# Turning two heads of k and q as 64x128 tiles beside the scores, in an attention and mixer kernel on one core

## The chip, the core and the metric

The kernel runs on one core of one Trainium2 chip. The metric is the time of one execution in microseconds, taken on the device. The text calls the core's engines by the names of the profile: PE multiplies matrices (PEld is its weight loads), DVE is the vector engine, ACT the scalar engine, POOL and SP issue most of the DMAs, and POOL does a little arithmetic as well.

## The reference

Eight batches of eight heads, 576 positions, 64 elements a head. Attention has a causal mask and a bias that falls with the running sum of `max(s, 0)`; a mixer over tokens and one over channels follow.

```python
scores = scale * np.matmul(q, k.transpose(0, 1, 3, 2))
cum = np.cumsum(np.maximum(s, 0.0), axis=-1)
bias = -(cum[:, :, :, None] - cum[:, :, None, :])
scores = np.where(causal, -1000000000.0, scores + np.minimum(bias, 0.0))
attn = softmax(scores)
x = heads side by side of np.matmul(attn, v)          # 8 x 576 x 512
h = np.maximum(x^T @ w_tok1, 0.0) @ w_tok2            # over tokens, 256 wide
u = x + h^T
out = u + np.maximum(u @ w_ch1, 0.0) @ w_ch2          # over channels, 1536 wide
```

## The kernel before

The bias is taken as a weight on v, `exp(cum)` of a position, so that a position's window of attention is its own block of 128 and the one before. A test at the end sets a flag for inputs where this does not hold; a general path, not taken here, would then compute everything anew.

**Stages of a batch.** Heads come in groups of four (`quad`, two groups a batch, numbered 0 to 15 in this text). k and q of a group are loaded as bf16 into a buffer of the ring `qkn` (5 buffers), two heads on the upper and two on the lower 64 partitions, 9 positions a partition. PE turns them: for k and then for q (`ti`), 9 slices x 2 halves x 2 heads, 36 transposes of 64x64 (line 706). Each result, two heads stacked on 128 partitions, is copied by ACT (line 718) or DVE (line 720) to `kT` or `qT`. A group has two pairs of heads (`pair`). A pair's scores are ten matmuls (line 750) on tiles of 64 rows and 128 columns, the two heads of the pair beside each other on the upper and the lower rows, in two pieces: 4 matmuls into one psc buffer and 6 into another. ACT exponentiates each piece (line 758), DVE masks it (lines 767 and 775), PE multiplies it with v (line 821), DVE divides (lines 850 and 854). When a batch has its eight heads, `tok` runs the token mixer (lines 921, 983) and turns its result: from batch 2 on by DMA transposes on SP's queue (line 999). `chan` runs the channel mixer (lines 1039 and 1064) with an evacuation by ACT (line 1046) or DVE (line 1048) per output of the first half, and stores each block.

**Buffers that PE writes.** `psc` has two buffers of 1024 columns, `pmx` four of 512. Before, the turns of batch 0 go to pmx, those of the other batches to one psc buffer for each `ti`; scores and attention times v use psc; both mixers use pmx.

**The order.** `Plan.op` records every piece of work with its engines, durations, priority, and what it reads, writes and holds. `Plan.run` then places them greedily: at each step it takes the engine that could start earliest, and on it, of the operations that could start within a small slack, the one with the lowest priority number. On PE it knows two shapes of tile: an operation with `mode=1` (turns and scores) has narrow tiles, and a change between narrow and full costs `SWITCH = 0.095` (line 17); while PE is in narrow shape, narrow work that is ready goes first. `after` makes an operation wait for the end of another on its engine. `late` and the `MARGIN` constants put a reserve between producer and consumer. The order found becomes the order of instructions of each engine, which the chip follows with semaphores. Up to `WARM` = 45 us, idle PE time is filled with matmuls on zeros (line 1160).

**Loads.** POOL issues the loads of k, q, v and weights in one chain (`load_op`), the first in a paced manner, by touching a piece of an earlier load (line 459). A load of k and q needs a free `qkn` buffer. At batch 5 (`B - 3`), POOL touches the turned input of the channel mixer before the loads of two batches' k and q come again for the sums of squares that the flag needs (`stage_sq`); the other batches' squares are ACT operations of low priority (line 664). The scan of line 1123 and the small operations behind it belong to that flag as well; they wait for the key `late`, set in `tok(0)`.

Of the kernel before, what the change touches and what calls it, by code (L numbers as in the profile page):

```python
# [237 lines left out]
def c_pe(n, f32=False):  # L238
    occ = n * (4 if f32 else 1) / 2400.0 + 0.0025
    return occ, occ + 0.21  # L240
# [131 lines left out]
def kernel(  # L372
# [22 lines left out]
    NQ = 512  # L395
    LAG = 2.5
    WARM = 45.0
    TOK = 2.0
    R = 9
    PR = S // R  # L400
# [9 lines left out]
    def ring(name, n, shape, dt, pool=None):  # L410
        p = pool or fast
        return Ring(name, [p.tile(shape, dt, name=f"{name}{i}", tag=f"{name}{i}") for i in range(n)])
# [17 lines left out]
        return EB[jc] + (64 if odd else 128) if jc == NJ - 2 else EB[jc] - (64 if odd else 0)  # L430

    r_qn = ring("qkn", 5, [128, 2, 2, R * D], BF16)
    r_qT = ring("qT", 4, [128, S], BF16)
    r_kT = ring("kT", 4, [128, 640], BF16)
    r_E = ring("E", 4, [128, 2, EW], BF16)
# [97 lines left out]
    for ti, src in enumerate((k, q)):  # L533
        def load0(ti=ti, src=src):
            nc.sync.dma_start(out=stage[:, ti, :, :],
                              in_=src[0, 0:4, :, :].rearrange("(f e) (p r) d -> (e p) f (r d)", e=2, r=R))
        P.op({"SP": (0.6, 4.0 + 0.9 * ti, load0)}, writes=[("stage", ti)], prio=-9 + ti)
        for f in range(2):
            def cast0(eng, ti=ti, f=f):
                if eng:  # L540
                    nc.vector.tensor_copy(out=first.t[:, ti, f, :], in_=stage[:, ti, f, :])
                else:
                    nc.scalar.copy(out=first.t[:, ti, f, :], in_=stage[:, ti, f, :])
            P.op({"ACT": (*c_act(576), lambda cast0=cast0: cast0(0)),
                  "DVE": (0.1 + 576 * 0.00104, 0.25 + 576 * 0.00104, lambda cast0=cast0: cast0(1))},
                 reads=[("stage", ti)], writes=[(first, ti, f)], prio=-6)
# [120 lines left out]
    def stage_qk(b, h):  # L667
        n = qkn[(b, h)] = Buf(r_qn)
        for i, src in enumerate((k, q)):
            load_cast(n, b, h, i, src)  # L670
        if b > 1:
            squares(b, h, n)
# [13 lines left out]
    xbuf = {}  # L686
    bd = Buf(r_mx, False)

    def quad(b, h):
        nat = qkn[(b, h)]  # L690
        np_ = (b * H + h) / 2
        dsts = [(Buf(r_kT), Buf(r_qT)) for e in range(2)]
        pads = [("pad", 2), ("pad", 3)] if b == 0 and h == 4 else []
        for ti in range(2):
            pts = [Buf(r_mx, False) for e in range(2)] if b == 0 else [Buf(r_sc, False)] * 2

            def pv(e, pts=pts):
                o = pts[e].t[:, :].bitcast(BF16)
                return o[:, 0:1024] if b == 0 else o[:, e * 1024 : e * 1024 + 1024]

            def tr(ti=ti, pv=pv):
                for r in range(R):
                    for e in range(2):
                        p0 = e * PR
                        for f in range(2):
                            nc.tensor.transpose(out=pv(e)[f * D : f * D + D, r * PR : (r + 1) * PR],  # L706
                                                in_=nat.t[p0 : p0 + PR, ti, f, r * D : (r + 1) * D],
                                                identity=ident[p0 : p0 + PR, p0 : p0 + PR])
            turn = P.op({"PE": (R * 0.031, R * 0.031 + 0.21, tr)}, reads=([(nat, ti, 0), (nat, ti, 1)] if b == 0 and h == 0 else [(nat, ti)]) + ["ident"] + pads,
                 writes=[(pts[e], e) for e in range(2)] + (["turned"] if b == 0 and h == 0 and ti == 0 else []), holds=[d[ti] for d in dsts], prio=(np_ - 30 * (b < 1 and h < 1), 2), mode=1)  # L710
            if b == 0 and h == 0 and ti == 1:
                scan.deps.add(turn)
            for e in range(2):
                def ev(eng, ti=ti, e=e, pv=pv):
                    i = pv(e)[:, 0:S].rearrange("d (r p) -> d p r", r=R)
                    o = dsts[e][ti].t[:, 0:S].rearrange("d (p r) -> d p r", r=R)
                    if eng == 0:
                        nc.scalar.copy(out=o, in_=i)  # L718
                    else:
                        nc.vector.tensor_copy(out=o, in_=i)  # L720
                P.op({"ACT": (*c_act(576), lambda ev=ev: ev(0)), "DVE": (*c_dve(576), lambda ev=ev: ev(1))},
                     reads=[(pts[e], e)], writes=[(dsts[e][ti], 0)], prio=1, alone=pts[e])
        for e in range(2):
            pair(b, h + e, *dsts[e])

    def pair(b, h, kT, qT):
        np_ = (b * H + h // 4 * 4) / 2 + h % 2
        E = Buf(r_E)
        odd = b % 2
        for pc, piece in enumerate(PIECES):  # L730
            ps = Buf(r_sc, False)
            c0 = 0
            cols = []
            for (jc, a, e) in piece:
                cols.append((jc, a, e, c0))
                c0 += e - a

            if b == 0:
                def preset(ps=ps, pc=pc):
                    for hh in range(2):  # L740
                        nc.tensor.matmul(out=ps.t[:, hh * 512 : hh * 512 + 512], lhsT=ident[:, :], rhs=neg[:, pc, :],  # L741
                                         start=True, stop=False)
                P.op({"PE": (2 * c_pe(512)[0], 2 * c_pe(512)[0] + 0.21, preset)}, reads=["neg", "ident"] + ["turned"],
                     writes=[(ps, 0)], prio=(np_ - 9, 0))

            def mm(ps=ps, cols=cols):
                for (jc, a, e, c0) in cols:
                    j0 = S - 128 if odd and jc == NJ - 1 else jc * 128
                    for hh in range(2):
                        nc.tensor.matmul(out=ps.t[:, hh * 512 + c0 : hh * 512 + c0 + e - a],  # L750
                                         lhsT=kT.t[hh * 64 : hh * 64 + 64, j0 : j0 + 128],
                                         rhs=qT.t[hh * 64 : hh * 64 + 64, a:e], start=b > 0, stop=b > 0 or jc == cols[-1][0])
            occ = sum(c_pe(e - a)[0] for (_, a, e, _) in cols)
            P.op({"PE": (occ, occ + 0.21, mm)}, reads=[(kT, 0), (qT, 0)], writes=[(ps, 0)], holds=[E], prio=(np_ - 9 * (b < 1), 1),
                 mode=1)

            def ex(ps=ps, pc=pc):
                nc.scalar.activation(out=E.t[:, :, 512 * pc : 512 * pc + 512],  # L758
                                     in_=ps.t[:, :].rearrange("p (e n) -> p e n", e=2), func=AF.Exp, scale=0.125)
            P.op(act(1024, ex), reads=[(ps, 0)], writes=[(E, jc) for (jc, a, e) in piece], prio=0)  # L760

            if b == 0:
                continue

            def mk(pc=pc):
                o = E.t[:, :, 512 * pc : 512 * pc + 512].rearrange("p e (c n) -> p e c n", c=2)[:, :, :, 0:128]
                nc.vector.tensor_tensor(  # L767
                    out=o, in0=o, in1=keep[:, :].unsqueeze(1).unsqueeze(1).to_broadcast([128, 2, 2, 128]), op=ALU.mult)
            P.op(dve(512, mk, True), reads=[(E, piece[0][0]), (E, piece[1][0]), "keep"],
                 writes=[(E, piece[0][0]), (E, piece[1][0])], prio=0, lock=True)  # L770
            if pc == 1:
                def mk4():
                    k0 = 64 if odd else 0
                    o = E.t[:, :, EB[4] : EB[4] + 64]
                    nc.vector.tensor_tensor(
                        out=o, in0=o, in1=keep[:, k0 : k0 + 64].unsqueeze(1).to_broadcast([128, 2, 64]), op=ALU.mult)
                P.op(dve(128, mk4, True), reads=[(E, 4), "keep"], writes=[(E, 4)], prio=0, lock=True)
# [117 lines left out]
    def tok(b):  # L895
# [80 lines left out]
        for c in range(NJ):  # L976
# [40 lines left out]
                else:  # L1017
                    nc.vector.tensor_copy(out=o, in_=i)
            P.op(either(512, lambda ev=ev: ev(0), lambda ev=ev: ev(1), True), reads=[(pt, 0)], writes=[(uT, c)], prio=0)
        if b == 0:  # L1020
            P.writer["late"] = P.ops[-1]
        return u, us, uT

# [80 lines left out]
    for i in range(2, 4):  # L1104
        load_ch2(i)
    stage_v(1)
    for b in range(2, B):
        stage_qk(b, 0)
        stage_v(b)
        stage_qk(b, 4)  # L1110
    for b in range(B):
        for h in range(0, H, 4):
            quad(b, h)
        st = tok(b)
        chan(b, *st)
        if b == B - 3:
            for c in range(NJ):
                touch(lambda c=c, uT=st[2]: uT.t[0:1, 0, c * 128 : c * 128 + 1], [(st[2], c)], 1)
            for i in range(2):
                for h in range(0, H, 4):  # L1120
                    stage_sq(i, h)
# [87 lines left out]
```

## Time and profile before

| | us |
|---|---|
| median of 3 runs | 303.14 |
| lowest and highest of them | 301.69 and 303.29 |
| the profiled execution, its own time | 302.87 |
| its span in the profile | 301.1 |
| PE busy in it | 292.5 |
| DVE, ACT, POOL busy | 187.5, 183.9, 80.6 |

The runs are timed from outside of the program, the span runs from the first to the last instruction of the profile. Rows of the timeline have the start, the length, the engine, the line, the operation, the tiles that it writes and reads, the tile shape of PE, the operand's size and how many instructions are merged. On PE the length takes in the pipeline's end of the last matmul, so what an instruction costs the stream is read from start to start. Groups of instructions have busy time and mean duration in ns of one.

### The profile page before, as it was taken

How to read it: one execution, taken by the hardware profiler on the slowest of the kernel's cores; microseconds unless marked ns; L12 is line 12 of the kernel's file. 1: busy time of each engine (PE TensorE's matmuls, PEld its weight loads, DVE VectorE, ACT ScalarE, POOL GpSimd, SP SyncE). 2: the span in 40 equal slices, each digit the busy share in tenths (PEclk: the TensorE clock that was granted, in tenths of full speed). 3: DMA queues.
4: the chain of work that ended last, by engine and by line, in shares of the span. 5: the costliest groups of instructions: out<-in, count | busy, mean ns of one | idle time of the engine just before them, and what ended most of it. 6: DMA issues, size and time to landing. Idle time of an engine off the chain costs nothing.

```text
span 301.1 us, 8152 instructions
## 1 busy us (share of the span) xinstructions
PE 292.5 (97%) x3432; PEld 168.0 (56%) x3432; DVE 187.5 (62%) x408; ACT 183.9 (61%) x300; POOL 80.6 (27%) x138
## 2 busy tenths in 40 slices
PE   8999999999999999999999999999999999999991
PEld 3478567576755455556754545447755444457550
DVE  5971889899987569756766548746868451520030
ACT  5778884779877678538792377128975275028300
POOL 8645678786630521007000000024100000000000
PEclk9999999999999999999999999999999999999998
DMA  7999989999999696258705200159635310250032
GB/s 213 227 206 207 210 191 235 189 241 229 203 235 162 154 227 108 65 137 194 121 2 105 108 35 2 54 140 184 106 67 101 110 37 0 71 159 0 4 112 68
DMA packets 38347, 39.28 MB, mean 130 GB/s; under 512 B 17600, under 2 KB 30976, under 8 KB 38304
## 3 DMA queue, kind: packets, MB, share of 16 engines
q0 software_dynamic: 17072, 24.25, 44.5%
q1 hardware_dynamic: 21232, 14.44, 18.5%
q8 instruction: 28, 0.46, 0.6%
q14 instruction: 15, 0.12, 0.1%
HBM read 40.65 MB, written 9.44 MB: 166 GB/s over the span
## 4 chain that ended last, share of the span: by engine, by line
PE 95%; DVE 1%; ACT 1%; issue 0%; DVEq 0%
PE pmx L1039 32%; PE pmx L1064 31%; PE psc L750 6%; PE pmx L983 6%; PE pmx L921 6%; PE psc L821 5%; PE psc L706 3%; PE pmx L1160 2%; PE psc L741 1%; ACT x L843 1%; PE pmx L706 1%; PE pmx L959 1%; DVE qT L720 0%; PE pmx L1008 0%; PE pmx L949 0%; DVE x L837 0%
## 5 line engine op out<-in xcount | busy, mean ns | idle before, releaser
L758 ACT ACTIVATE E<-psc 128x1024 bf16<-128x1024 f32 x64 | 62.2, 1022 | 29.0 <-PE psc L750 28.5
L1039 PEld LDWEIGHTS <-wc 128*128 128x128 bf16 x624 | 58.0, 98 | 31.2 <-issue 1.1
L1039 PE MATMUL pmx<-uTb,wc 128*128 128x320 bf16 (+2 forms) x384 | 55.6, 299 | 0.0
L1064 PE MATMUL pmx<-wc,gb 128*128 128x512 bf16 (+1 forms) x252 | 54.7, 369 | 0.0
L1039 PE MATMUL pmx<-uTa,wc 128*128 128x512 bf16 (+1 forms) x240 | 45.6, 337 | 0.0
L1064 PE MATMUL pmx<-wc,ga 128*128 128x512 bf16 x192 | 44.6, 379 | 0.0
L664 ACT ACTIVATE junk<-qkn 128x1152 bf16<-128x1152 bf16 x32 | 37.3, 1165 | 4.3 <-DMA qkn<-in_q_dram 3.9
L1064 PEld LDWEIGHTS <-gb 128*128 128x128 bf16 x252 | 23.7, 98 | 25.1
L1046 ACT ACTIVATE gb<-pmx 128x320 bf16<-128x320 f32 (+2 forms) x53 | 23.0, 436 | 20.0 <-PE pmx L1039 16.1
L630 POOL DMA_DIRECT2D vf<-in_v_dram x39 | 33.4, 870 | 4.6 <-issue 2.0
L767 DVE TENSOR_TENSOR E<-E,keep 128x512 bf16<-128x512 bf16 x56 | 22.9, 416 | 10.9 <-ACT E L758 10.7
L1064 PEld LDWEIGHTS <-ga 128*128 128x128 bf16 x192 | 18.1, 98 | 20.2 <-issue 0.2
L1046 ACT ACTIVATE ga<-pmx 128x512 bf16<-128x512 f32 (+1 forms) x43 | 22.8, 535 | 10.3 <-PE pmx L1039 9.5
L648 DVE TENSOR_TENSOR vp<-vf,wT 128x512 bf16<-128x512 f32 (+1 forms) x39 | 25.5, 686 | 1.5 <-DMA vf<-in_v_dram 1.3
L1048 DVE TENSOR_SCALAR gb<-pmx 128x320 bf16<-128x320 f32 (+2 forms) x43 | 20.9, 490 | 5.4 <-PE pmx L1039 4.3
L821 PEld LDWEIGHTS <-E 128*128 128x128 bf16 x576 | 21.1, 97 | 5.5
L718 ACT COPY kT<-psc 128x576 bf16<-128x576 bf16 x21 | 12.7, 642 | 18.4 <-PE psc L706 18.2
L854 DVE TENSOR_TENSOR x<-psc,rc 128x640 bf16<-128x640 f32 x28 | 23.0, 823 | 0.9
L1072 DVE TENSOR_TENSOR of<-pmx,ua 128x512 f32<-128x512 f32 x16 | 11.0, 688 | 18.0 <-PE pmx L1064 15.4
L479 POOL DMA_DIRECT2D qkn<-in_k_dram x19 | 13.8, 728 | 30.7 <-PE psc L706 14.5
L750 PE MATMUL psc<-qT,kT 64*128 64x256 bf16 (+2 forms) x320 | 21.8, 250 | 0.0
L479 POOL DMA_DIRECT2D qkn<-in_q_dram x19 | 13.7, 722 | 28.3 <-PE psc L706 25.4
(110 smaller groups left out, 300.0 us busy)
## 6 DMA issues: line engine op xcount, KB each, us to landing
vf<-in_v_dram POOLq DMA_DIRECT2D x32, 256.0 KB, 7.8
out_dram<-of SPq DMA_DIRECT2D x31, 256.0 KB, 2.2
qkn<-in_k_dram POOLq DMA_DIRECT2D x19, 288.0 KB, 7.1
qkn<-in_q_dram POOLq DMA_DIRECT2D x19, 288.0 KB, 7.6
wc<-in_moe_w_ch_dram POOLq DMA_DIRECT2D x8, 384.0 KB, 8.3
out_dram<-of SPq DMA_DIRECT2D x10, 128.0 KB, 2.3
vf<-in_v_dram POOLq DMA_DIRECT2D x7, 128.0 KB, 7.7
gb<-in_k_dram SPq DMA_DIRECT2D x1, 576.0 KB, 4.1
```

Of the source, the lines that this page charges most:

```text
L479: nc.gpsimd.dma_start(out=n.t[:, i, :, :], in_=src[b, h : h + 4, :, :].rearrange("(f e) (p r) d -> (e p) f (r d)", e=2, r=R))
L630: nc.gpsimd.dma_start(out=vf.t[p0 : p0 + n, c, :, :], in_=v[b, :, c * 128 : c * 128 + n, :].rearrange("h p d -> p h d"))
L648: eng.tensor_tensor(out=vp.t[p0 : p0 + n, c, :, 0:D], in0=vf.t[p0 : p0 + n, c, :, :], in1=wT[p0 : p0 + n, cw, b * H : b * H + H].unsqueeze ...
L664: nc.scalar.activation(out=junk[:, :].rearrange("p (t n) -> p t n", t=2), in_=i, func=AF.Square, accum_out=sq[:, col : col + 1])
L750: nc.tensor.matmul(out=ps.t[:, hh * 512 + c0 : hh * 512 + c0 + e - a], lhsT=kT.t[hh * 64 : hh * 64 + 64, j0 : j0 + 128], rhs=qT.t[hh * 64 ...
L758: nc.scalar.activation(out=E.t[:, :, 512 * pc : 512 * pc + 512], in_=ps.t[:, :].rearrange("p (e n) -> p e n", e=2), func=AF.Exp, scale=0.125)
L767: nc.vector.tensor_tensor(out=o, in0=o, in1=keep[:, :].unsqueeze(1).unsqueeze(1).to_broadcast([128, 2, 2, 128]), op=ALU.mult)
L821: nc.tensor.matmul(out=o[:, ic, 0:DE], lhsT=E.t[:, hh, d0 : d0 + 128], rhs=vp.t[:, jc, h + 2 * hh, 0:DE], start=(jc == j_lo), stop=(jc == ic))
L854: nc.vector.tensor_tensor(out=x.t[:, :, :].rearrange("p c (g f e d) -> p g e f c d", f=2, e=2, d=D)[:, h // 4, h % 2], in0=pav2()[:, :, :, ...
L1039: nc.tensor.matmul(out=pm.t[:, 0 : e - a], lhsT=wc1[:, m, cc * 128 : cc * 128 + 128], rhs=uT.t[:, m, a:e], start=(m == 0), stop=(m == NMC ...
L1046: lambda cc=cc, pm=pm, a=a, e=e: nc.scalar.activation(out=g.t[:, cc, a:e], in_=pm.t[:, 0 : e - a], func=AF.Relu),
L1064: nc.tensor.matmul(out=pm.t[:, na:ne], lhsT=g.t[:, cc, c * 128 : c * 128 + 128], rhs=wc2[:, cc, na:ne], start=(cc == 0), stop=(cc == NCC - 1))
```

## The change

A new ring `qk` has two buffers. From batch 1 on, the k and then the q of a group are first copied, by ACT or DVE, from `qkn` into such a buffer with the two heads of each half side by side: the copy has 1152 elements a partition. A turn then takes 9 slices x 2 halves, 18 transposes of 64x128, and gives the same stacked result. The very first group is cast into that layout directly and turned so as well; the second group of batch 0 keeps its 36.

From batch 1 on (`BOTH = 2`), the two pieces of a pair's scores are one operation of PE, and need both psc buffers at once. From batch 2 on (`JOIN = 4`), a turn goes to two pmx buffers, and it may start only after the scores of the pair of the same number in the group before: k behind the first pair, q behind the second, with about the priority of those scores.

The scan of line 1123 waits for batch 4 in place of batch 0. The loads are issued in the old order up to v of batch 5; those of the second group of batch 5 and of batch 6 come behind touches of batch 2's turned input, those of batch 7 behind touches of batch 3's.

```diff
+    JOIN = 4
+    BOTH = 2
...
+    r_qk = ring("qk", 2, [128, R, 2, D], BF16)
...
             def cast0(eng, ti=ti, f=f):
+                o = first.t[:, ti, :, :].rearrange("p f n -> p (f n)").rearrange("p (r f d) -> p r f d", r=R, f=2)[:, :, f, :]
+                i = stage[:, ti, f, :].rearrange("p (r d) -> p r d", r=R)
                 if eng:
-                    nc.vector.tensor_copy(out=first.t[:, ti, f, :], in_=stage[:, ti, f, :])
+                    nc.vector.tensor_copy(out=o, in_=i)
                 else:
-                    nc.scalar.copy(out=first.t[:, ti, f, :], in_=stage[:, ti, f, :])
+                    nc.scalar.copy(out=o, in_=i)
...
+    scores = {}
+
     def quad(b, h):
         nat = qkn[(b, h)]
+        gi = 2 * b + h // 4
+        join = gi >= JOIN
...
-            pts = [Buf(r_mx, False) for e in range(2)] if b == 0 else [Buf(r_sc, False)] * 2
-
-            def pv(e, pts=pts):
+            apart = b == 0 or join
+            pts = [Buf(r_mx, False) for e in range(2)] if apart else [Buf(r_sc, False)] * 2
+
+            def pv(e, pts=pts, apart=apart):
                 o = pts[e].t[:, :].bitcast(BF16)
-                return o[:, 0:1024] if b == 0 else o[:, e * 1024 : e * 1024 + 1024]
+                return o[:, 0:1024] if apart else o[:, e * 1024 : e * 1024 + 1024]
+
+            if b == 0 and h == 0:
+                skey = [(nat, ti, 0), (nat, ti, 1)]
+            elif b:
+                qk = Buf(r_qk, False)
+
+                def turn_in(eng, ti=ti, qk=qk):
+                    o = qk.t[:, :, :, :].rearrange("p r f d -> p f r d")
+                    i = nat.t[:, ti, :, :].rearrange("p f (r d) -> p f r d", r=R)
+                    if eng:
+                        nc.vector.tensor_copy(out=o, in_=i)
+                    else:
+                        nc.scalar.copy(out=o, in_=i)
+                P.op({"ACT": (*c_act(1152), lambda t=turn_in: t(0)), "DVE": (*c_dve(1152, True), lambda t=turn_in: t(1))},
+                     reads=[(nat, ti)], writes=[(qk, 0)], prio=20, lock=True).late = 6
+                skey = [(qk, 0)]
+            else:
+                skey = [(nat, ti)]
+            wide = b > 0 or h == 0
+
+            def tr_wide(ti=ti, pv=pv, qk=qk if b else None):
+                t = (nat.t[:, ti, :, :].rearrange("p f n -> p (f n)").rearrange("p (r n) -> p r n", r=R) if b == 0 else
+                     qk.t[:, :, :, :].rearrange("p r f d -> p r (f d)"))
+                for r in range(R):
+                    for e in range(2):
+                        p0 = e * PR
+                        nc.tensor.transpose(out=pv(e)[:, r * PR : (r + 1) * PR], in_=t[p0 : p0 + PR, r, :],
+                                            identity=ident[p0 : p0 + PR, p0 : p0 + PR])
...
-            turn = P.op({"PE": (R * 0.031, R * 0.031 + 0.21, tr)}, reads=([(nat, ti, 0), (nat, ti, 1)] if b == 0 and h == 0 else [(nat, ti)]) + ["ident"] + pads,
-                 writes=[(pts[e], e) for e in range(2)] + (["turned"] if b == 0 and h == 0 and ti == 0 else []), holds=[d[ti] for d in dsts], prio=(np_ - 30 * (b < 1 and h < 1), 2), mode=1)
+            turn = P.op({"PE": (R * 0.029, R * 0.029 + 0.21, tr_wide if wide else tr)}, reads=skey + ["ident"] + pads,
+                 writes=[(pts[e], e) for e in range(2)] + (["turned"] if b == 0 and h == 0 and ti == 0 else []), holds=[d[ti] for d in dsts],
+                 prio=(np_ - 2 + ti, 2) if join else (np_ - 30 * (b < 1 and h < 1), 2), mode=1, after=scores[gi - 1, ti] if join else None)
...
+        gi = 2 * b + h // 4
+        both = gi >= BOTH
+        todo, pieces = [], []
         for pc, piece in enumerate(PIECES):
...
-            occ = sum(c_pe(e - a)[0] for (_, a, e, _) in cols)
-            P.op({"PE": (occ, occ + 0.21, mm)}, reads=[(kT, 0), (qT, 0)], writes=[(ps, 0)], holds=[E], prio=(np_ - 9 * (b < 1), 1),
-                 mode=1)
+            pieces.append(ps)
+            todo.append((ps, sum(c_pe(e - a)[0] for (_, a, e, _) in cols), mm))
+            if both and pc == 0:
+                continue
+
+            def mms(todo=tuple(todo)):
+                for t in todo:
+                    t[2]()
+            occ = sum(t[1] for t in todo)
+            scores[gi, h % 2] = P.op(
+                {"PE": (occ, occ + 0.21, mms)}, reads=[(kT, 0), (qT, 0)], writes=[(t[0], 0) for t in todo], holds=[E],
+                prio=(np_ - 9 * (b < 1), 1), mode=1)
+            todo = []
...
-        if b == 0:
+        if b == 4:
             P.writer["late"] = P.ops[-1]
...
-    for b in range(2, B):
+
+    def stage_in(b):
         stage_qk(b, 0)
         stage_v(b)
         stage_qk(b, 4)
+
+    def behind(b, uT):
+        for c in range(NJ - 1 + b % 2):
+            touch(lambda c=c: uT.t[0:1, 0, c * 128 : c * 128 + 1], [(uT, c)], 1)
+    for b in range(2, 5):
+        stage_in(b)
+    stage_qk(5, 0)
+    stage_v(5)
     for b in range(B):
         for h in range(0, H, 4):
             quad(b, h)
         st = tok(b)
         chan(b, *st)
+        if b == 2:
+            behind(b, st[2])
+            stage_qk(5, 4)
+            stage_in(6)
+        if b == 3:
+            behind(b, st[2])
+            stage_in(7)
         if b == B - 3:
-            for c in range(NJ):
-                touch(lambda c=c, uT=st[2]: uT.t[0:1, 0, c * 128 : c * 128 + 1], [(st[2], c)], 1)
+            behind(b, st[2])
             for i in range(2):
                 for h in range(0, H, 4):
                     stage_sq(i, h)
```

More of the change, by code (lines that the diff above doesn't have):

```diff
@@ L752, in mm @@
                                          rhs=qT.t[hh * 64 : hh * 64 + 64, a:e], start=b > 0, stop=b > 0 or jc == cols[-1][0])
-            occ = sum(c_pe(e - a)[0] for (_, a, e, _) in cols)
-            P.op({"PE": (occ, occ + 0.21, mm)}, reads=[(kT, 0), (qT, 0)], writes=[(ps, 0)], holds=[E], prio=(np_ - 9 * (b < 1), 1),
-                 mode=1)
+            pieces.append(ps)
[10 more added lines that the diff above has]
+            todo = []
+        for pc, piece in enumerate(PIECES):
+            ps = pieces[pc]
             def ex(ps=ps, pc=pc):
```

## The prediction

> **What bounds the kernel now.** I read the page first (shares, chain), then the waits of PE, then the table of stretches, then the timeline of PE around a few head groups.
>
> ```profile
> span 301.1 us, 8152 instructions
> ...
> PE 292.5 (97%) x3432; PEld 168.0 (56%) x3432; DVE 187.5 (62%) x408; ACT 183.9 (61%) x300; POOL 80.6 (27%) x138
> ...
> PE 95%; DVE 1%; ACT 1%; issue 0%; DVEq 0%
> ```
>
> The chain that ended last is 95% PE. A busy PE may still be a PE that stands, so the waits of PE come next, between 28 us, where the filled start is over, and 294 us, where the chain leaves PE for the last output, and with them the busy time of the engines that serve it:
>
> ```profile
> 294.36 0.42 DVE of L1072
> ```
> ```profile
> PE pmx L921 <- issue: 0.2, 1, 0.2
> ```
> ```profile
> 28.00:60.00 32.00, 31.75 (x505) 19.87 (x504) 26.26 (x62) 24.37 (x41) 23.91 (x45) 1.00 1.07 206
> 60.00:80.00 20.00, 19.96 (x285) 14.19 (x284) 18.86 (x43) 16.82 (x29) 13.60 (x21) 1.00 1.10 227
> 80.00:100.00 20.00, 20.00 (x227) 10.32 (x229) 14.77 (x32) 14.28 (x23) 4.67 (x6) 1.00 1.21 204
> 100.00:135.00 35.00, 35.00 (x475) 17.82 (x470) 24.57 (x48) 22.78 (x34) 7.82 (x10) 1.00 0.64 134
> ```
>
> The columns are stretch, length, then busy time of PE, PEld, DVE, ACT and POOL, granted clock, DMA share, GB/s. PE waits once, for 0.2 us, in 266 us, and the granted clock is 1.00. So PE's instruction stream itself is the time: what is taken out of it comes off the end, as long as nobody makes PE wait instead. DVE and ACT are free enough from 80 us on (about two thirds to three quarters busy), but together 89% busy from 60 to 80 us.
>
> What the stream pays apart from streaming shows only in start times:
>
> ```profile
> 107.93 0.39 PE L750 MATMUL psc<-qT,kT 64*128 64x256 bf16 x4
> 108.25 1.04 PE L1039 MATMUL pmx<-uTa,wc 128*128 128x512 bf16 x4
> 109.22 0.40 PE L750 MATMUL psc<-qT,kT 64*128 64x256 bf16 x6
> 109.55 0.48 PE L706 MATMUL psc<-ident,qkn 64*64 64x64 bf16 x36
> 109.96 2.76 PE L1039 MATMUL pmx<-uTa,wc 128*128 128x512 bf16 x12
> 112.56 0.71 PE L821 MATMUL psc<-vp,E 128*128 128x65 bf16 x18
> 113.10 1.89 PE L1039 MATMUL pmx<-uTa,wc 128*128 128x512 bf16 x8
> 114.92 0.80 PE L706 MATMUL psc<-ident,qkn 64*64 64x64 bf16 x72
> 115.65 1.90 PE L1039 MATMUL pmx<-uTa,wc 128*128 128x512 bf16 x8
> 117.49 0.61 PE L750 MATMUL psc<-qT,kT 64*128 64x256 bf16 x10
> 118.03 2.33 PE L921 MATMUL pmx<-x,w 128*128 128x512 bf16 x10
> 120.20 2.75 PE L1064 MATMUL pmx<-wc,ga 128*128 128x512 bf16 x12
> ```
>
> Ten full matmuls of 512 columns take 118.03 to 120.20, 0.217 us each. Eight take 1.736; but from 115.65 to the scores at 117.49 it is 1.84, so 0.10 goes to the change from tile shape 128*128 to 64*128. From 113.10 to the turns at 114.92 it is 1.82, 0.08 for the change to 64*64. The ten score matmuls run two beside each other, 1024 columns in all, 0.434 us by the same rate; 117.49 to 118.03 is 0.54, so 0.106 goes to the change back. I take 0.095 us for each change of shape; it is also the constant `SWITCH` of line 17.
>
> **The count of changes.** The timeline of PE has its first and last burst of narrow tiles behind 28 us here:
>
> ```profile
> 28.45 0.48 PE L706 MATMUL psc<-ident,qkn 64*64 64x64 bf16 x36
> ...
> 168.72 0.80 PE L706 MATMUL psc<-ident,qkn 64*64 64x64 bf16 x72
> ...
> 245.30 0.77 PE L750 MATMUL psc<-qT,kT 64*128 64x256 bf16 x10
> ```
>
> Counted between them: 8 turn bursts x36 and 9 x72 by themselves; 2 turn bursts x36 right behind scores (109.55 is one); and 34 score bursts, because 6 of the 28 head pairs are cut into x4 and x6 as at 107.93 and 109.22. That is 51 bursts, 102 changes, and 2 inner changes: 104, or 9.9 us.
>
> **The change part by part.**
>
> (a) Both pieces of scores become one operation from batch 1 on, and a turn of the groups from batch 2 on is put behind the scores of the pair before it, in the same 64*128 shape. If all goes so, 28 score bursts are left, 24 turns lie inside them, and only the 4 turns of batch 1 stand alone: 32 bursts, 64 changes. Removed: 40 x 0.095 = 3.8 us. A turn now needs two of the four pmx buffers free at the very moment that the scores end, and its copies ready; else PE takes other work and the turn comes alone, for 0.19. I let one in six fail: 4 x 0.19 = 0.76 back. Bounds: none (0) and all 24 (4.6).
>
> (b) A turn has 18 transposes in place of 36. The 36 of 109.55 take until 109.96, less the change back, 0.315 us. Two of the new ones lie beside each other as the scores do, 64 columns long. The trace has no such stream; the nearest is line 821, where a full 128-column weight load and a 65-column matmul come every 0.030 us (18 in 112.56 to 113.10). Nine pairs: 0.27, so 0.045 less each, 28 turns: 1.2 us. Bounds: at best the columns alone, 9 x 0.027 = 0.24, 2.1 us; at worst the weight load's whole duration, below.
>
> ```profile
> L750 PEld LDWEIGHTS <-kT 64*128 64x128 bf16 x320 | 12.5, 94 | 14.8 <-issue 12.1 <-ACT qT L718 0.5 <-ACT ga L1046 0.4
> ```
>
> If loads did not overlap, a pair would cost 94 ns, a turn 0.85, and 28 turns 15 us more. I take 0.030, since line 821's loads are as long in their records and still follow each other at that pace. The Trainium skill ("TensorE: Matmul & The Clock Gate", LDWEIGHTS) prices a load by its columns over 1.2 GHz: 107 ns for 128, twice that of 64, which is against this change; by it, an estimate, 28 turns of 9 x 0.107 would cost 18 us more. This case's line 821 does not bear it out as a spacing, with 0.030 us for a load of 128.
>
> (c) New are 28 copies of 1152 elements (`turn_in`), on DVE or ACT.
>
> ```profile
> L664 ACT ACTIVATE junk<-qkn 128x1152 bf16<-128x1152 bf16 x32 | 37.3, 1165 | 4.3 <-DMA qkn<-in_q_dram 3.9
> L767 DVE TENSOR_TENSOR E<-E,keep 128x512 bf16<-128x512 bf16 x56 | 22.9, 416 | 10.9 <-ACT E L758 10.7
> L1123 DVE TENSOR_TENSOR_SCAN pre<-one_sb,wn 64x576 f32<-64x576 f32 x1 | 1.3, 1339 | 0.0
> ```
>
> ACT passes over the same shape in 1.165; DVE by line 767 scaled needs 0.416 x 1152/512 = 0.94. Say 1.05 each, 29 us over both. Cover: about 10 fall between 28 and 80 us, where DVE and ACT idle 104 - 86.3 = 17.7 us together; 10.5 of that goes, and the scan of line 1123, moved behind batch 4, gives 1.3 back. Those engines then stand at about 92%, and evacuations that PE waits for come later. Without the cover half of 10.5, 5 us, would be on the path. Behind 80 us there is room. For all new stalls I take 0.7 us, nearer to the one wait of 0.2 above than to 5. The copies also free the qkn buffers, for which loads waited on the turns; no load was late for PE, so no gain.
>
> (d) The turned tiles of the later groups are evacuated from pmx, not psc, by the same copies as before:
>
> ```profile
> L718 ACT COPY kT<-psc 128x576 bf16<-128x576 bf16 x21 | 12.7, 642 | 18.4 <-PE psc L706 18.2
> L720 DVE COPY qT<-psc 128x576 bf16<-128x576 bf16 x11 | 8.0, 753 | 0.9 <-PE psc L706 0.5
> L758 ACT ACTIVATE E<-psc 128x1024 bf16<-128x1024 f32 x64 | 62.2, 1022 | 29.0 <-PE psc L750 28.5
> ```
>
> The q of a group is turned behind the last scores of the group before. From there to its own first scores the old order leaves at least 8 us (109.22 to 117.49), and two copies of 0.75 need 1.5. Nothing is taken for this; what it can do is the first rival.
>
> (e) Loads held: POOL touches the turned inputs of batches 2 and 3 (4 and 5 small casts) before the loads of groups 11 to 13 and 14 to 15 with their v. Queued behind are only loads, and the copies of group 11 wait for them.
>
> ```profile
> L999 SPq DMA_TRANSPOSE uTa<-ua x12: 1196/1216/1333, 90.6 to 231.6; - x12
> L999 SPq DMA_TRANSPOSE uTb<-ub x12: 1189/1202/1211, 125.3 to 263.7; - x12
> ```
> ```profile
> qkn<-in_q_dram POOLq DMA_DIRECT2D x19, 288.0 KB, 7.6
> ```
>
> Batch 2 is turned from 90.6 us on, so the loads go at about 100 and have landed near 110; group 11 is turned at 168.72. Batch 3 follows at 125, its loads are there near 150, and the group is wanted behind 200. Cost 0, with 50 us in hand. A faster DMA transpose brings nothing either, for PE does not wait for one.
>
> (f) The first group's casts write 64-element runs, and its turns are wide. The casts could become 0.1 us slower or the turns 0.1 faster, four times over; 0.
>
> **Sum:** -3.8 + 0.76 - 1.2 + 0.7 = -3.5 on the profiled 302.87 (span 301.1 with 1.8 around it) gives 299.3. That execution is 0.27 below the median of 303.14, so I say 299.5.
>
> **The rivals.**
>
> Evacuation becomes the bound (slower). A turn holds two of four pmx buffers just as two exponentials of 1.022 us fall due on ACT. Its two copies (0.64 to 0.75) queue with them, and the channel matmuls behind have two buffers left, filled every 0.54 us (four of 320 columns) and emptied in 0.49. For it: 24 such places. Against it: at 109.96 twelve matmuls behind scores and a turn take 2.60 = 12 x 0.217, no stall; but that turn was in psc. At 0.35 us a place it costs 8.4 against 5.0 gained: 306.3. It eats the gain from 0.21 us a place, and shows as slower from 0.27.
>
> The turns don't attach (the change doesn't do what it says). Then 24 turns stand alone, 48 changes in place of 28 (13 bursts and 2 inner changes), the cuts give 12 back: 8 x 0.095 = 0.76 more, less 1.2 of (b), 0.7 of stalls: 303.1, the same.
>
> The wide turns are bound by weight loads: 94 ns a pair gives +15 and -3.0 for fewer changes, about 315. Line 821 speaks against it.
>
> **How the numbers follow.** Forecast 0.64; evacuation 0.17; no attachment 0.14; weight loads 0.04; the rest is a stall early that eats the gain. The forecast's own range is 297.4 (5.0 gained, no stall, and the lower runs of before) to 301.5 (stalls near 3). To hold 8 in 10 it has to reach over the second rival: 297.4 to 304.0, which leaves out most of evacuation and the weight loads. About 0.5%, 1.5 us, is what a measurement here can tell from no change: faster (below 301.6) has the forecast and 0.02 of the second rival, 0.66; same the rest of that and the mild end of the first, 0.16; slower 0.18.
>
> **What would show it.** Right: 64*128 bursts of 28 (10 scores and 18 transposes) with one change each side, about 32 to 36 narrow bursts behind 28 us, a turn of about 0.27 us, PE's waits still under 1 us. (a) fails if turns of 18 stand between 128*128 rows; (b) if 18 take over 0.315; (c) and (d) if PE waits behind copies or evacuations, by stretch 28 to 80 or behind bursts; (e) if DVE or ACT waits for a qkn load behind 160 us. The forecast is wrong if PE idles for over 3 us in all.

## The result, and the profile after

The changed kernel takes 298.37 us (median of 6 runs, 298.18 to 298.49) against 302.87 (6 runs, 301.69 to 303.29): a ratio of 0.9857, interval 0.9838 to 0.9876. The profiled execution took 298.18 with a span of 296.2. The forecast was 299.5, between 297.4 and 304.0, and faster.

The page of the changed kernel, its head and its chain:

```profile
span 296.2 us, 7117 instructions
...
PE 285.4 (96%) x2860; PEld 168.1 (57%) x2893; DVE 201.6 (68%) x434; ACT 191.9 (65%) x303; POOL 81.8 (28%) x146
...
PE 91%; DMA 2%; DVE 2%; ACT 1%; issue 1%; POOL 0%; POOLq 0%; DVEq 0%
```

PE is the bound as before, while DVE and ACT got 14 and 8 us more of busy time. PE's own is 7.1 us less, more than the 4.9 by which the span shrank: PE has 33 records fewer than PEld has weight loads. Where a matmul's record is missing, two starts lie one matmul further apart (0.217 us for 512 columns), which is no stall. The waits of PE in the changed kernel between 28 and 290 us:

```profile
PE pmx L975 <- ACT h L987: 0.2, 1, 0.2
PE pmx L1118 <- issue: 0.2, 1, 0.2
```

The second of them, behind the turn at 167.06, is as long as one missing record and counts as none. And the same stretches as before, with the same columns:

```profile
28.00:60.00 32.00, 31.45 (x398) 20.54 (x401) 27.38 (x59) 26.95 (x44) 22.39 (x42) 1.00 1.06 206
60.00:80.00 20.00, 19.87 (x281) 14.49 (x280) 18.66 (x44) 18.12 (x28) 11.73 (x18) 1.00 1.08 225
80.00:100.00 20.00, 19.84 (x182) 10.26 (x185) 17.40 (x35) 19.25 (x33) 8.39 (x14) 1.00 0.86 173
```

DVE and ACT now stand at 85% from 28 to 60 us and at 92% from 60 to 80, 88% over both. The timeline of PE in the changed kernel has turns that stand alone, up to 68.38, and from 70.18 on turns inside the scores' burst:

```profile
65.84 0.44 PE L736 MATMUL pmx<-ident,qk 64*128 64x64 bf16 x18
66.30 2.14 PE L1093 MATMUL pmx<-uTb,wc 128*128 128x256 bf16 x16
68.38 0.44 PE L736 MATMUL pmx<-ident,qk 64*128 64x64 bf16 x18
68.79 1.46 PE L1093 MATMUL pmx<-uTb,wc 128*128 128x384 bf16 x8
70.18 0.61 PE L792 MATMUL psc<-qT,kT 64*128 64x256 bf16 x10
70.63 0.43 PE L736 MATMUL pmx<-ident,qk 64*128 64x64 bf16 x18
```
```profile
125.80 0.59 PE L1118 MATMUL pmx<-wc,ga 128*128 128x512 bf16 x2
126.33 0.61 PE L792 MATMUL psc<-qT,kT 64*128 64x256 bf16 x10
126.78 0.43 PE L736 MATMUL pmx<-ident,qk 64*128 64x64 bf16 x18
127.14 1.68 PE L1118 MATMUL pmx<-wc,ga 128*128 128x512 bf16 x6
```

From 126.33 to the turn at 126.78 is 0.45: ten scores and no change of shape behind them (before, 0.54 with one). From 126.78 to 127.14 is 0.36: a turn of 0.265 and the one change back.

Adding up, over the records of single matmuls, the time from each start to the next gives where PE's stream got shorter. It is taken from the first channel matmul (25.30 us before, 25.25 after) to PE's last one (294.28 and 289.68); 0.094 us is put aside for each change of shape. What a burst of turns or scores takes over the median of its kind, or a full matmul over the usual distance of its size, counts as a stall if it is over 0.03 us and no missing record:

| us of PE's stream | before | after | difference | forecast |
|---|---|---|---|---|
| changes of shape, 105 and 75 | 9.87 | 7.05 | -2.8 | -3.0 |
| turns | 8.91 | 7.49 | -1.4 | -1.2 |
| scores | 12.71 | 12.60 | -0.1 | 0 |
| stalls | 1.17 | 0.96 | -0.2 | +0.7 |
| full-shape work | 236.32 | 236.32 | 0 | 0 |
| sum | 268.98 | 264.43 | -4.55 | -3.5 |

Of the stalls before, 0.53 lie inside three score bursts of ten that look whole on PE's timeline: their second piece waits. One of them, before:

```profile
244.79 0.82 DVE L854 TENSOR_TENSOR x<-psc,rc 128x640 bf16<-128x640 f32 x1
245.30 0.77 PE L750 MATMUL psc<-qT,kT 64*128 64x256 bf16 x10
245.67 0.22 PEld L750 LDWEIGHTS <-kT 64*128 64x128 bf16 x5 [0.16 <-issue]
```

Here the second piece starts at 245.67, when DVE's divide at 244.79 has ended and given a psc buffer back. As one operation that needs both buffers, no pair of the changed kernel behind batch 0 stands like this.

Most of the rest of the 4.9 us by which the span shrank lies behind PE's last matmul (6.8 us before, 6.5 after).

### The profile page after: what moved, and what is told of

It reads as the page before. It is cut to its first block, busy times and chain, and to the rows that moved or that the text cites. A ratio compares the mean times of both kernels' runs of the same rounds, so it can differ in the third digit from the quotient of the medians.

```text
span 296.2 us, 7117 instructions
## 1 busy us (share of the span) xinstructions
PE 285.4 (96%) x2860; PEld 168.1 (57%) x2893; DVE 201.6 (68%) x434; ACT 191.9 (65%) x303; POOL 81.8 (28%) x146
## 4 chain that ended last, share of the span: by engine, by line
PE 91%; DMA 2%; DVE 2%; ACT 1%; issue 1%; POOL 0%; POOLq 0%; DVEq 0%
PE pmx L1093 32%; PE pmx L1118 31%; PE pmx L1037 6%; PE psc L792 6%; PE pmx L975 6%; PE psc L875 5%; DMA qkn<-in_k_dram 2%; PE pmx L736 2%; DVE qT L759 1%; ACT x L897 1%; PE psc L783 1%; PE pmx L1013 1%; PE psc L736 0%; PE pmx L744 0%; PE pmx L1003 0%
## 5 line engine op out<-in xcount | busy, mean ns | idle before, releaser
L1118 PE MATMUL pmx<-wc,gb 128*128 128x512 bf16 (+1 forms) x243 | 53.9, 369 | 0.6 <-issue 0.2
L1093 PE MATMUL pmx<-uTa,wc 128*128 128x512 bf16 (+1 forms) x235 | 44.8, 336 | 0.3
L1100 ACT ACTIVATE gb<-pmx 128x320 bf16<-128x320 f32 (+2 forms) x51 | 22.1, 437 | 18.3 <-PE pmx L1093 15.0
L1100 ACT ACTIVATE ga<-pmx 128x512 bf16<-128x512 f32 (+1 forms) x48 | 24.8, 526 | 12.8 <-PE pmx L1093 12.0
L653 DVE TENSOR_TENSOR vp<-vf,wT 128x512 bf16<-128x512 f32 (+1 forms) x40 | 26.5, 681 | 1.3 <-DMA vf<-in_v_dram 0.9
L462 POOL CAST seen<-uTb 1x1 f32<-1x1 bf16 x10 | 2.3, 235 | 81.2 <-DMA uTb<-ub 79.5
L821 DVE TENSOR_TENSOR E<-E,keep 128x512 bf16<-128x512 bf16 x56 | 22.0, 415 | 1.4 <-ACT E L812 1.4
L792 PEld LDWEIGHTS <-kT 64*128 64x128 bf16 x320 | 12.9, 94 | 13.7 <-issue 12.0
L792 PE MATMUL psc<-qT,kT 64*128 64x256 bf16 (+2 forms) x320 | 20.3, 250 | 0.3
L875 PE MATMUL psc<-vp,E 128*128 128x65 bf16 x522 | 20.3, 193 | 0.0
```

Source lines behind the costliest of these rows:

```text
L653: eng.tensor_tensor(out=vp.t[p0 : p0 + n, c, :, 0:D], in0=vf.t[p0 : p0 + n, c, :, :], in1=wT[p0 : p0 + n, cw, b * H : b * H + H].unsqueeze ...
L821: nc.vector.tensor_tensor(out=o, in0=o, in1=keep[:, :].unsqueeze(1).unsqueeze(1).to_broadcast([128, 2, 2, 128]), op=ALU.mult)
L875: nc.tensor.matmul(out=o[:, ic, 0:DE], lhsT=E.t[:, hh, d0 : d0 + 128], rhs=vp.t[:, jc, h + 2 * hh, 0:DE], start=(jc == j_lo), stop=(jc == ic))
L1093: nc.tensor.matmul(out=pm.t[:, 0 : e - a], lhsT=wc1[:, m, cc * 128 : cc * 128 + 128], rhs=uT.t[:, m, a:e], start=(m == 0), stop=(m == NMC ...
L1100: lambda cc=cc, pm=pm, a=a, e=e: nc.scalar.activation(out=g.t[:, cc, a:e], in_=pm.t[:, 0 : e - a], func=AF.Relu),
L1118: nc.tensor.matmul(out=pm.t[:, na:ne], lhsT=g.t[:, cc, c * 128 : c * 128 + 128], rhs=wc2[:, cc, na:ne], start=(cc == 0), stop=(cc == NCC - 1))
```

## The experiments

**The theory**: on a PE that never waits, each change of tile shape costs 0.094 us, and the programs' own counts of changes give the differences between them. **Rivals**: the shorter turns bring the gain; the gap at a change is no cost of the change but that of a new burst's first data; the copies cost DVE and ACT what PE gains. The counts in the expectations are from the order of PE's instructions in each program, behind the first channel matmul. All times are medians of runs made beside runs of the kernel before.

| run | us | ratio to before | interval | changes |
|---|---|---|---|---|
| changed kernel | 298.37 | 0.9857 | 0.9838 to 0.9876 | 75 |
| turns not joined | 300.08 | 0.9928 | 0.9907 to 0.9950 | 95 |
| scores cut | 301.33 | 0.9958 | 0.9938 to 0.9977 | 87 |
| old turns, joined | 303.19 | 1.0020 | 1.0004 to 1.0036 | 90 |
| wide turns alone | 301.54 | 0.9973 | 0.9960 to 0.9986 | 103 |
| loads not held | 312.07 | 1.0307 | 1.0277 to 1.0336 | 75 |
| batch 1 joined too | 300.79 | 0.9932 | 0.9905 to 0.9959 | 71 |
| copies doubled | 301.07 | 0.9941 | 0.9920 to 0.9962 | 75 |
| copies on DVE | 298.81 | 0.9871 | 0.9846 to 0.9897 | 69 |
| full shape between | 302.94 | 1.0020 | 1.0003 to 1.0036 | 113 |
| turn shape between | 298.82 | 0.9876 | 0.9850 to 0.9901 | 75 |
| first try at a better one | 298.51 | 0.9866 | 0.9838 to 0.9893 | 75 |
| second try | 297.34 | 0.9826 | 0.9801 to 0.9852 | 71 |

**The price of a change by itself.** One extra matmul between the scores and each joined turn, once of the full shape and once of the turn's shape; nothing else in the order moves, and the turn overwrites what it wrote.

```diff
+                if join:
+                    for p0 in (0,):
+                        nc.tensor.matmul(out=pts[0].t[:, 0:64], lhsT=ident[0:128, :], rhs=ident[0:128, 0:64], start=True, stop=True)
```
```diff
+                        nc.tensor.matmul(out=pts[0].t[:, 0:64], lhsT=ident[p0:p0+64, :], rhs=ident[p0:p0+64, 0:64], start=True, stop=True)
```

> The changed kernel with one extra full-shape matmul of 64 columns on the identity between the scores and each joined turn (24 of them, overwritten by the turn; the order of everything else is left as it is). It breaks each joined burst in two: 113 changes against 75. Theory: +38 x 0.094 = 3.6, + 24 x 0.03 for the matmul itself = 0.7, so 302.7, between 302.2 and 303.2. Rival (a change of shape by itself is hidden, the gap seen at it is that of a first instruction in a burst, which waits for its data): + 0.7 alone, 299.1.

> As the run with an extra full-shape matmul between scores and joined turn, but the extra matmul has the shape of the turn, 64x128 with 64 columns (24 of them): 75 changes of shape, the burst is not broken. Theory: 298.4 + 24 x 0.029 = 299.1, between 298.6 and 299.5; the run with the full shape stands 3.8 above it. Rival (an extra instruction there costs, whatever its shape): as that run, 302.9.

Measured 302.94 and 298.82, both inside their ranges and 4.1 apart, where 38 changes at 0.094 make 3.6; by this pair a change costs 0.108. A burst of the first on the timeline of PE, then one of the second:

```profile
127.72 0.61 PE L795 MATMUL psc<-qT,kT 64*128 64x256 bf16 x10
128.26 0.20 PE L735 MATMUL pmx<-ident 128*128 128x64 bf16 x1
128.40 0.43 PE L739 MATMUL pmx<-ident,qk 64*128 64x64 bf16 x18
128.76 0.61 PE L1121 MATMUL pmx<-wc,ga 128*128 128x512 bf16 x2
```
```profile
126.59 0.61 PE L795 MATMUL psc<-qT,kT 64*128 64x256 bf16 x10
127.04 0.19 PE L735 MATMUL pmx<-ident 64*128 64x64 bf16 x1
127.04 0.45 PE L739 MATMUL pmx<-ident,qk 64*128 64x64 bf16 x18
127.42 1.90 PE L1121 MATMUL pmx<-wc,ga 128*128 128x512 bf16 x8
```

From scores to the next full matmul it is 1.04 in the first and 0.83 in the second, with the same work. The data were there in both, so the 0.2 belongs to the two more changes. The rival of first data falls.

**Parts of the change.** Turns not joined: `JOIN = 99`. Wide turns alone: `JOIN = 99` and `BOTH = 99`. Scores cut: `BOTH = 99`.

> The changed kernel with JOIN = 99: turns wide and copied, scores whole, but no turn is put behind scores (turns of batch 1 on go to psc again). Theory (each change of tile shape costs 0.094 us of PE's stream, and nothing else matters): its program has 95 changes behind the first channel matmul where the changed kernel has 75, so 298.4 + 20 x 0.094 = 300.3, between 299.9 and 300.7. Rival (the gain came from the wide turns and from the copies that free buffers; where a turn stands is indifferent): 298.4 within 0.4. Rival (joining costs stalls in pmx): below 298.4.

> The changed kernel with JOIN = 99 and BOTH = 99: only the wide turns, the copies, and the held loads. Theory: 103 changes against 105 of before, so of the gain only the shorter turns are left: before (302.9) - 0.2 - 1.2 + 0.3 = 301.8, between 301.2 and 302.3. Rival (wide turns bring most): 299 to 300. Rival (copies cost what the turns bring): 302.9.

> The changed kernel with BOTH = 99: the two pieces of a pair's scores are separate operations again, turns still joined. 87 changes of shape against 75, 6 pairs cut. Theory: 298.4 + 12 x 0.094 = 1.1, and 0.1 for each cut itself (the scores stream was 13.20 with six cuts in the run with wide turns alone, 12.60 in the changed kernel) = 0.6, so 300.1, between 299.6 and 300.7. Rival (the order that needs both psc buffers at once makes waits of its own, so cutting is free): 298.4 to 299.

The first two came as expected, 300.08 and 301.54: 20 more changes cost 1.7 (1.9 by count), and the wide turns with everything that they need bring about 1.2 of the 4.5. So the rival that the shape of the turn brings most falls. Between these two, whole scores bring 1.5: 8 changes fewer are 0.75, and four waits between the pieces of a pair, 0.67 in all, are gone. The third missed its range, 301.33 in place of 300.1. Its stream is 2.0 longer: 1.1 for changes, 0.1 for scores and 0.8 more of stalls (1.8 in all, three of them of 0.34 to 0.39 us between 57 and 67 us, and 0.34 between the pieces of two pairs). The expectation had put 0.1 on each cut by itself; but a cut pair takes only 0.014 more than a whole one, whose ten matmuls take 0.449, so that term was such waits, misread. Another 0.35 lies behind PE's last matmul, which with the 2.0 makes the 2.3 between the profiled executions (300.50 and 298.18); the 3.0 between the medians is more because this profiled execution is 0.8 below its median. A different order of operations brought its own stalls, which a count of changes does not see.

**The old turns, joined.** No copies, and 36 transposes read from `qkn`:

```diff
-            elif b:
+            elif False:
...
-            wide = b > 0 or h == 0
+            wide = b == 0 and h == 0
```

> The changed kernel, but from batch 1 on without copies, and each turn again 36 transposes of 64x64 read from qkn, still put behind the scores where there is room. Theory: a turn behind scores has a change inside the burst; the program has 90 changes against 75, +1.4 us, and 28 turns are 0.05 us longer, +1.4, less up to 0.3 for copies that are gone: 300.9, between 300.3 and 301.4. Rival (joining alone, whatever the shape, brings the gain): 298.4 to 299. Rival (the copies cost a lot on DVE and ACT, hidden in the sum): below 298.4.

Measured 303.19, over the range, 0.2% above the kernel before. Of the 4.7 us that its stream is longer than the changed kernel's, the records find 1.4 in changes, 1.5 in turns and 2.0 in stalls (3.0 in all: 2.1 between 50 and 64 us, 0.6 between 68 and 92), with 0.2 less elsewhere. Against the kernel before, 15 changes fewer save 1.4 and stalls that are 1.8 longer eat it. So joining without the new shape brought nothing in this order, and the rival that joining alone brings the gain falls; that it could bring nothing in an order without those stalls is not shown. Taking the copies out does not make the early stretch easier here, since the order is another.

**The copies.** Each made twice, and planned so; then all on DVE at a planned 0.5 us; then the turns of batch 1 joined as well (`JOIN = 2`).

```diff
+                    for _ in range(2):
+                        if eng:
+                            nc.vector.tensor_copy(out=o, in_=i)
+                        else:
+                            nc.scalar.copy(out=o, in_=i)
...
-                P.op({"ACT": (*c_act(1152), lambda t=turn_in: t(0)), "DVE": (*c_dve(1152, True), lambda t=turn_in: t(1))},
+                P.op({"ACT": (*c_act(2304), lambda t=turn_in: t(0)), "DVE": (*c_dve(2304, True), lambda t=turn_in: t(1))},
```
```diff
+                P.op({"DVE": (0.5, 0.62, lambda t=turn_in: t(1))},
```

> The changed kernel with each of the 28 copies made twice, and planned so; 75 changes of shape. The profile has 17 copies of 1.16 us on ACT and 11 of 0.45 to 0.5 on DVE, so about 25 us more of engine time. Theory (copies lie in idle time of DVE and ACT, PE does not see them): 298.4 to 299.1. Rival (between 28 and 80 us the two engines are at their end, as the prediction had it as bound): a tenth of them on the path or more, 301 or more, with stalls of PE before 80 us.

> The changed kernel with the 28 copies on DVE alone, planned at 0.5 us (measured 0.45 to 0.5 there, 1.16 on ACT). Its program has 69 changes of shape against 75. Theory: 298.4 - 6 x 0.094 = 297.8, between 297.4 and 298.2; ACT is freed of 20 us, which brings nothing by itself. Rival (ACT is what the early stretch waits for): below 297.4. Rival (DVE becomes late): 298.6 or more.

> The changed kernel with JOIN = 2: the turns of batch 1 are put behind scores as well. 71 changes of shape against 75. Theory: 298.4 - 4 x 0.094 = 298.0, between 297.6 and 298.4. Rival (in the early stretch DVE and ACT can't take two exponentials and two copies at once): 298.8 or more, with stalls before 60 us.

All three missed, on the same side, and where the rival that each names had put them. Doubled copies give 301.07, 2.7 over the changed kernel. Groups of the changed kernel, then of the run with doubled copies:

```profile
L722 ACT COPY qk<-qkn 128x1152 bf16<-128x1152 bf16 x17 | 19.7, 1161 | 0.1
L720 DVE COPY qk<-qkn 128x1152 bf16<-128x1152 bf16 x11 | 5.5, 500 | 2.6 <-DMA qkn<-in_k_dram 1.4 <-DMA qkn<-in_q_dram 1.1
```
```profile
L723 ACT COPY qk<-qkn 128x1152 bf16<-128x1152 bf16 x26 | 30.0, 1156 | 0.4
L721 DVE COPY qk<-qkn 128x1152 bf16<-128x1152 bf16 x30 | 14.9, 496 | 1.8 <-DMA qkn<-in_k_dram 1.3
```

That is 19.7 us more of engine time for 2.7 us on the path. The waits of PE with doubled copies, 28 to 290 us:

```profile
PE pmx L1063 <- ACT uTb L1071: 0.5, 1, 0.5
PE pmx L737 <- ACT gb L1101: 0.4, 1, 0.4
PE psc L876 <- DVE x L909: 0.3, 1, 0.3
PE pmx L1094 <- DVE kT L760: 0.2, 1, 0.2
...
```

PE waits for evacuations by ACT and DVE, and by the records 3.2 of its 3.4 us of stalls lie between 51 and 80 us. So the cover of the copies is nearly used up there, and whole behind it: the theory that PE does not see them holds only behind 80 us. With all copies on DVE the 6 changes saved (0.56) were eaten by stalls between 51 and 67 us (2.2 in all, against 1.0). With batch 1 joined, PE stood between 49 and 53 us:

```profile
47.82 1.25 PE L875 MATMUL psc<-vp,E 128*128 128x65 bf16 x36
49.34 0.44 PE L736 MATMUL pmx<-ident,qk 64*128 64x64 bf16 x18 [0.27 <-DVE qk L720]
50.43 0.44 PE L736 MATMUL pmx<-ident,qk 64*128 64x64 bf16 x18 [0.66 <-ACT qk L722]
52.11 1.02 PE L1118 MATMUL pmx<-wc,ga 128*128 128x512 bf16 x3 [1.24 <-ACT kT L757]
```
```profile
49.22 1.15 ACT L722 COPY qk<-qkn 128x1152 bf16<-128x1152 bf16 x1 [1.25 <-DMA qkn<-in_q_dram]
```

First it waits for the copies themselves, the second of which stood for its load, then for the evacuation of kT. DVE is busy 4.00 and ACT 3.78 of the 4 us from 49 to 53. So this is the first rival of the prediction, in a place where the engines are full, and in part a load that lands late.

**The held loads.** All loads in the old order, no touches:

```diff
-    for b in range(2, 5):
+    for b in range(2, B):
         stage_in(b)
-    stage_qk(5, 0)
-    stage_v(5)
...
-        if b == 2:
-            behind(b, st[2])
-            stage_qk(5, 4)
-            stage_in(6)
-        if b == 3:
-            behind(b, st[2])
-            stage_in(7)
```

> The changed kernel with all loads of k, q and v in the old order and not held behind the turned inputs of batches 2 and 3. 75 changes of shape, as the changed kernel. Theory (the loads have tens of us in hand, PE waits for no DMA): 298.4, within 0.4. Rival (the hold keeps loads off the DMA transposes, which the channel mixer waits for): 299.2 or more, with waits on uTa or uTb in the profile.

Measured 312.07, 13.7 over the changed kernel: the rival holds, and by far more than it asked. The profiled execution is the slowest of the six, 315.60 and so 17.4 over that of the changed kernel. PE's longest wait in this run, and the time to landing of its DMA transposes in us:

```profile
PE pmx L1093 <- DMA uTa<-ua: 14.0, 1, 14.0
```
```profile
DMA to landing us min/median/max: 2.4/2.8/20.9
```

Behind that wait PE runs at a granted clock of 0.51 for some 5 us, which makes the loss longer than the wait (columns as in the stretches above):

```profile
117.00:122.00 5.00, 4.61 (x27) 2.33 (x28) 1.75 (x4) 0.00 (x0) 0.00 (x0) 0.51 0.78 196
```

The transposes of batch 2 are issued from 90.78 us on. POOL's loads around them, in this run:

```profile
87.90 0.72 POOL L482 DMA_DIRECT2D qkn<-in_q_dram  x1
89.78 0.70 POOL L482 DMA_DIRECT2D qkn<-in_k_dram  x1 [1.16 <-ACT junk L669]
90.47 0.71 POOL L482 DMA_DIRECT2D qkn<-in_q_dram  x1
91.18 0.90 POOL L635 DMA_DIRECT2D vf<-in_v_dram  x1
```

and in the kernel before:

```profile
85.64 0.72 POOL L479 DMA_DIRECT2D qkn<-in_q_dram  x1 [0.70 <-DMA qkn<-in_k_dram]
100.89 0.71 POOL L479 DMA_DIRECT2D qkn<-in_k_dram  x1 [14.54 <-PE psc L706]
```

Before, the next load stood 14.54 us, until PE had turned group 7 out of its buffer; that chance wait kept the transposes free. With the copies the buffer is free earlier, nothing stops the loads, and they run beside the transposes. The touches put the stop back. In the changed kernel the loads go on behind the last of them, and a transpose lands in 4.4 us at most:

```profile
97.47 0.17 POOL L462 CAST seen<-uTa 1x1 f32<-1x1 bf16 x1 [1.13 <-DMA uTa<-ua]
97.98 0.71 POOL L482 DMA_DIRECT2D qkn<-in_k_dram  x1 [0.34 <-issue]
```
```profile
DMA to landing us min/median/max: 2.4/2.5/4.4
```

**A better version.** Two tries, both with copies on DVE alone from an early group on, a planned 0.5 us there and a reserve of 10 us (`late = 10`). The first does so from group 5 on and leaves `JOIN = 4`; the second from group 4 on, with `JOIN = 6`:

```diff
-    JOIN = 4
+    JOIN = 6
...
-                P.op({"ACT": (*c_act(1152), lambda t=turn_in: t(0)), "DVE": (*c_dve(1152, True), lambda t=turn_in: t(1))},
-                     reads=[(nat, ti)], writes=[(qk, 0)], prio=20, lock=True).late = 6
+                P.op({"DVE": (0.5, 0.62, lambda t=turn_in: t(1))} if gi >= 4 else {"ACT": (*c_act(1152), lambda t=turn_in: t(0)), "DVE": (0.5, 0.62, lambda t=turn_in: t(1))},
+                     reads=[(nat, ti)], writes=[(qk, 0)], prio=20, lock=True).late = 10
```

> The changed kernel with the copies from group 5 on on DVE alone, planned at 0.5 us on DVE everywhere, and with a reserve of 10 us behind the load in place of 6. 75 changes, but its order leaves ACT freer between 55 and 80 us, where the stalls of PE have shown. Theory (the stalls of 0.9 us there are engine load): 297.4 to 298.1. Rival (those stalls have another cause): 298.4 or more.

> The changed kernel with JOIN = 6 (the turns of batch 2 stand where they did), copies from group 4 on on DVE alone, planned at 0.5 us, and a reserve of 10 us. 71 changes of shape against 75. Theory: 298.4 - 0.4 and less of the stalls of 0.9 us: 297.3 to 298.1. Rival (DVE becomes late between 50 and 70 us, as with all copies on DVE): 298.8 or more.

The first missed and came where its rival had it (298.51, stalls of 1.0 us, most at the same places as in the changed kernel); the second came as expected: 297.34, with 71 changes and 0.65 us of stalls. It beats the kernel before clearly; that it beats the changed kernel, 1.0 us by the medians, is likely but not settled, since the intervals of the two ratios overlap.

## Why the prediction was right, and where it was not

- What bounds the kernel: right. PE's stream set the time before and after, and what left it came off the end.
- (a) changes: right. 30 went where 32 were forecast (40 less 4 times 2); 5 of 24 turns stand alone, not 4, all of them up to 93 us. With the 4 of batch 1 that makes 37 narrow bursts, one over the 32 to 36 that the prediction named as its sign. Each change costs about 0.1: 0.094 by the start times, 0.108 by the pair of runs with an extra matmul.
- (b) turns: right, -1.4 for -1.2. A pair takes 0.029 (0.265 over nine), so the weight load does not bind, and the rival of weight loads falls with it.
- What the sum left out: a pair's second piece could wait for its psc buffer in the middle of a burst, 0.53 in three pairs before. The prediction shows one, the scores at 245.30 with 0.77 in place of 0.61, but went by the list of PE's waits, where it is not. A cut itself costs hardly more than its two changes, 0.014 a pair.
- (c) copies: the time on ACT was right, on DVE twice too long: 0.45 to 0.5 in place of 0.94, which had been scaled from a two-input operation. The Trainium skill ("VectorE: DVE Perf Modes", Side-by-side: where the cycles go for N=2048 bf16) has some 150 cycles and a quarter of a cycle for each bf16 element of a copy at 0.96 GHz, an estimate of 456 ns for 1152. The median of line 720 in this case's trace, 454 ns, bears that out. The step that was mis-sized most is the +0.7 for stalls: it was -0.2, for the 0.53 between pieces went and the others rose by 0.3. That DVE and ACT would be near their end from 28 to 80 us was right (88% for the 92% worked out), and the runs with doubled copies and with batch 1 joined show how near.
- (d) taking nothing for the evacuation was right: behind 80 us no stall stands at an attached turn. The rival that it becomes the bound did not come there; in the run with batch 1 joined it came in part, before 60 us.
- (e) held loads: the 0 against the kernel before was right, the reason was wrong. The step that failed is "A faster DMA transpose brings nothing either, for PE does not wait for one", and with it that freed buffers cost nothing: it read the waits of the old order as if they would hold in the new one. By the traces, PE did not wait because the buffers' wait held the loads; without the touches the changed kernel takes 13.7 us more.
- "The turns don't attach" came out cheaper than worked out: 300.08 in place of 303.1, because the order then pairs turns (9 bursts of 36, 95 changes) where 24 single ones were reckoned.
- (f) the first group's wide casts and turns at 0: nothing speaks against it, the first channel matmul starts at 25.25 for 25.30. They were not tried alone, and neither was the scan moved behind batch 4.
- The sum came out low in gain, 1.1 us by the forecast time and 1.4 by the two profiles (4.9 for 3.5): 0.9 of it in stalls, 0.3 behind the last matmul, 0.2 in turns and 0.1 in scores, less 0.2 in changes. So the two terms that carry the forecast, (a) and (b), were right by themselves and not by errors that cancel.

## What to carry to other kernels

Where one engine never waits, read its stream from start to start: what is not streaming there (here about 0.1 us at each change of tile shape) can be counted in the program and comes off the end, as long as the order that takes it out brings no stalls of its own: with the old turns joined, with batch 1 joined and with all copies on DVE it did. A buffer that is freed earlier also lets go what waited for it, so ask what that wait kept away, and put the stop back by name. And a cover of idle time has to be read by stretch: 20 us more of copies cost 2.7 us here, nearly all of it in the 30 us where both helping engines were almost full (90% busy from 51 to 80 us).

## What the runs showed of the hardware that was not expected

DMA transposes between on-chip buffers, which land in 2.4 us, took up to 20.9 when POOL's loads were issued in the same microseconds. A copy of 1152 bf16 elements a partition took 0.45 us on DVE and 1.16 on ACT. Transposes of 64x128, two beside each other and each with its own weight load, keep 0.029 us a pair (18 in 0.265 us), where 64 columns at the rate of 512 in 0.217 us would take 0.027. A change of tile shape costs PE about 0.1 us. After 14 us without work PE ran at a granted clock of 0.51 for some 5 us, and at 1.00 again from 122 us on.
